# Turning a mixture layer's results with TensorE instead of with a transposing DMA

## The chip, the cores and the metric

The kernel runs on one core of a Trainium2 chip. The metric is the device time of one execution in microseconds (us); lower is better. Times "of a run" are medians of several executions of the same kernel; the profile is one further execution.

## The reference

Windowed attention with 4 batches, 8 heads, 576 positions and a head dimension of 64 gives 2304 rows of 512 values. Two mixture layers follow. In each a row picks one of 8 experts by the largest of its router logits, goes through that expert's two matrices, and is scaled by its gate:

```python
logits = x @ w_gate                      # layer 2: + modality_bias[modality_id]
e_idx = np.argmax(logits, axis=1)
...
h = np.maximum(x[mask] @ w1[e], 0.0)     # 512 -> 1024
ye = h @ w2[e]                           # 1024 -> 512
out[mask] = gate_w[mask, None] * eom[mask, e, None] * ye   # layer 2: without eom
```

The second layer's router needs the first layer's result of each row, so every result of layer 1 is also multiplied by the second `w_gate`. All products run on pairs of float16 values (a high and a low part), which keeps float32 accuracy.

## The kernel before

After attention the rows are sorted by expert into **slots** of 128 rows that share one expert. Each mixture layer is a loop over slots (`moe`, `slot(s)`); 18 slots are always there, up to 9 more run if the sort fills them. In the profiled execution slots 0 to 22 of layer 1 ran, and then the second layer's slots.

The order of all work is written out by hand: what the program says first on an engine runs first there, and each engine waits for its own next instruction. In a slot of layer 1 this order is:

- SyncE (SP) issues the loads of the next experts' weights into a float32 buffer `raw` (line 91) as soon as the splits of earlier pieces have read it. The loads are conditional: they move data only where the expert changes.
- ScalarE (ACT) splits the high part of the weights (line 99) and VectorE (DVE) the low part (line 104) into one of two buffers `wb`. A slot has four such places, `sp(0)` to `sp(3)`.
- `post.out(s - 1, py)` takes the previous slot's product out of PSUM: ACT scales it into `y` (line 996) and casts its high half into the tile `y16` (line 997), GpSimd (POOL) copies the row numbers (line 990) and subtracts for the low half (line 998). There is one `y16` for all slots but slot 1.
- TensorE (PE) makes the first product, `mm1` (line 797): twice 48 matmuls, each group into its own bank. After the first group SP gets `post.transposes(s - 1)`: a transposing DMA of `y16` into `yT` (line 1003) and a DMA of `y16` to the DRAM table `y_dram` (line 1004), out of which layer 2 gathers its rows. Behind them stands the transposing DMA of the next slots' inputs, `xT` (line 770).
- PE makes the second product, `mm2` (line 864), 12 float16 and 8 float32 matmuls, and then the router of an older result (`post.router`, line 1017, 12 small matmuls out of `yT`): in slots up to 16 that of two slots ago, from slot 17 on that of the slot before. DVE adds it to the logits (line 1025).

`post.transposes(None)` for the very last slot of layer 1 already turns with PE: eight transposes of 128x128 into the PSUM tile `pyt` (line 1008) and one DVE copy into `yT` (line 1009). The PSUM tag `pyt` has one buffer; the search for layer 2's first expert (`first_expert`, its `pfe2` tile, written at the end of slot 3 and read by DVE lines 169 and 170 in slot 4) uses it too.

`Fill` (lines 914 to 941) loads and splits, from slot 5 to 16, the first expert of layer 2 in the gaps. `hook(k)` are the places where such side work is hung in.

Of the kernel before, what the change touches and what calls it, by code (L numbers as in the profile page):

```python
# [20 lines left out]
N, DM, E, F = 2304, 512, 8, 1024  # L21
# [8 lines left out]
CA1, CA2, CF = 13, 13, 4  # L30
KA, KE = 2, 3
NMIN = 18
NB = 12
BIG = 8e12
SQK = 2.0 ** 5
# [13 lines left out]
def fused(ctx, tc, qk, vw, wr1, w1a, w2a, mid, wr2, mbias, w1b, w2b, cf, c16, cbs, cms, cib, out, dbg=None):  # L49
    nc = tc.nc  # L50
# [26 lines left out]
    def plain(wb):  # L77

        return [wb[:, i, UF * 512:].bitcast(F32) for i in range(2)]

    def load_raw(w1, w2, ev, cond=None, pieces=range(8), wb=None):

        kw = {} if cond is None else dict(cond=cond, cond_hint=False)
        for k in pieces:
            if k < 4:
                src = w1[bass.ds(ev, 1), k * P:(k + 1) * P, :].rearrange("e p f -> p (e f)")
                d = raw[:, k * 1024:(k + 1) * 1024]
            else:
                src = w2[bass.ds(ev, 1), 2 * (k - 4) * P:2 * (k - 3) * P, :].rearrange("e (c p) f -> p (e c) f", p=P)
                d = (raw[:, k * 1024:(k + 1) * 1024] if wb is None else plain(wb)[k - UF // 2]).rearrange("p (c f) -> p c f", c=2)  # L90
            nc.sync.dma_start(d, src, **kw)
# [484 lines left out]
    vt, gt = nc.vector, nc.gpsimd  # L576
# [173 lines left out]
    def moe(w1, w2, tab, src, parts, post, start, wfirst):  # L750


        xg, xs, regs, evr = {}, {i: xsA[i] for i in range(KA)}, [], {}
        one = post is post1
        npc = UF // 2 if one else 8
        py = pp.tile([P, DM], F32, name="py", tag="py")
        pys = [pp.tile([P, DM], F32, name=f"pya{i}", tag=f"pya{i}") for i in range(KA)]

        def gather(s):
            if s >= NSLOT:  # L760
                return
            t = xgb[s % 3][:, 0:src.shape[1]]
            nc.gpsimd.indirect_dma_start(t, None, src, bass.IndirectOffsetOnAxis(start.idx[:, s:s + 1], 0))  # L763
            xg[s] = t

        def x_transpose(s):
            if s >= NSLOT:
                return
            g = xg.pop(s)
            nc.sync.dma_start(xsb[s % 3], g[:, 0:8 * P], transpose=True)  # L770
            xs[s] = xsb[s % 3]
            post.gathered(s, g)

        def weights(s, pieces=range(8), always=False):
            if s >= NSLOT:
                return
            if not regs or regs[2] != s:
                regs[:] = (nc.sync.value_load(tab[0:1, 0, s:s + 1], min_val=0, max_val=E - 1),
                           None if always else nc.sync.value_load(tab[0:1, 1, s:s + 1], min_val=0, max_val=1), s)
                evr[s] = regs[0]  # L780
            load_raw(w1, w2, regs[0], cond=regs[1], pieces=[k for k in pieces if k < npc])

        def plains(s):

            if s < NSLOT and one:
                c = None if s < KE + 2 else nc.sync.value_load(tab[0:1, 2, s:s + 1], min_val=0, max_val=1)
                load_raw(w1, w2, evr.pop(s), cond=c, pieces=range(npc, 8), wb=wbuf[s % 2])

        def mm1(g, w1h, w1l, xT, mid):
            ph = pp.tile([P, 4, P], F32, name=f"ph{g}", tag=f"ph{g}")  # L790
            k = 0
            for w, b_ in ((w1h, (0, 4)), (w1l, (0,))):
                for j in range(4):
                    fs = slice((4 * g + j) * P, (4 * g + j + 1) * P)
                    for c in range(4):
                        for i in b_:
                            nc.tensor.matmul(ph[:, j, :], w[:, c, fs], xT[:, parts[c + i], :], start=k == 0, stop=k == 47, skip_group_check=True)  # L797
                            k += 1
                if k == 32:
                    mid()  # L800
            return ph

        def hsplit(g, ph, hh, hl):
            if one and g == 1:
                nc.scalar.activation(hh, ph, AF.Relu, scale=SW)  # L805
                return
            hs = hh[:, 4 * g:4 * g + 4, :]
            nc.scalar.activation(hs, ph, AF.Relu)  # L808
            nc.vector.scalar_tensor_tensor(out=hl[:, 4 * g:4 * g + 4, :], in0=ph, scalar=0.0, in1=hs, op0=ALU.max, op1=ALU.subtract)  # L809

        def slot(s):
            wb = wfirst if s < KE else wbuf[s % 2]
            w1h, w1l = (wb[:, i, 0:4096].rearrange("p (c f) -> p c f", c=4) for i in range(2))
            w2h, w2l = (wb[:, i, 4096:].rearrange("p (c f) -> p c f", c=8) for i in range(2))
            xT = xs.pop(s)

            def sp(i):
                if KE <= s < NSLOT - 1:
                    splits(wbuf[(s + 1) % 2], MO['ta1' if one else 'ta'][i], lambda k: weights(s + 2, k))

            def hook(k):
                start.hook(s, k)

            if s >= KE:
                gather(s + 2)
            hh = mp.tile([P, 8, P], F16, name="hh")
            hl = mp.tile([P, 8, P], F16, name="hl")
            if one:

                hf, hl = hl.rearrange("p f t -> p (f t)").bitcast(F32).rearrange("p (f t) -> p f t", f=4), hh[:, 4:8, :]  # L830
                if s >= KE - 1:
                    plains(s + 1)
            hook(0)
            sp(0)
            if s >= KE:
                post.out(s - 1, py)
            if s >= NMIN - 1 and post is not post1:
                post.now(s)
            sp(1)
            ph0 = mm1(0, w1h, w1l, xT, lambda: hook(1))  # L840
            hook(2)
            if s == NMIN - 1:
                post.router(s - 2)
            if s >= KE:
                post.transposes(s - 1)
            if s >= KA:
                x_transpose(s + 2)
            hsplit(0, ph0, hh, hl)
            sp(2)
            hook(3)  # L850
            ph1 = mm1(1, w1h, w1l, xT, lambda: hook(4))
            hsplit(1, ph1, hf if one else hh, hl)
            hook(5)
            sp(3)
            k = 0
            to = pys[s] if s < KA else py
            if one:
                wf = [t.rearrange("p (f d) -> p f d", d=DM) for t in plain(wb)]
                ops = [(hh[:, f, :], w[:, f, :]) for f in range(4) for w in (w2h, w2l)] + [(hl[:, f, :], w2h[:, f, :]) for f in range(4)]
                ops += [(hf[:, f, :], wf[f // 2][:, f % 2, :]) for f in range(4)]  # L860
            else:
                ops = [(a[:, f, :], w[:, f, :]) for a, b_ in ((hh, (w2h, w2l)), (hl, (w2h,))) for f in range(8) for w in b_]
            for a, w in ops:
                nc.tensor.matmul(to, a, w, start=k == 0, stop=k == len(ops) - 1)  # L864
                k += 1
                if k == 12:
                    hook(6)
            if s >= NMIN - 1:
                post.router(s - 1)
            elif s >= KE - 1:  # L870
                post.router(s - 2)
            hook(7)

        start.gather, start.transpose, start.weights, start.pys = gather, x_transpose, weights, pys
        start.first_splits = lambda o: splits(wbuf[KE % 2], o, lambda k: weights(KE + 1, k))
        for s in range(NMIN):
            slot(s)
            if s == KE - 1:
                nsl = nc.values_load(tab[0:1, 0, 31:32], min_val=1, max_val=NSLOT)
        with ExitStack() as ifs:  # L880
            for s in range(NMIN, NSLOT):
                ifs.enter_context(tc.If(nsl > s))
                slot(s)
        return py
# [60 lines left out]
    class Start1(Start):  # L945
# [16 lines left out]
        def zero(self, i):  # L962

            nc.sync.dma_start(y_dram[(NMIN + i) * P:(NMIN + i + 1) * P, :], zt)

# [12 lines left out]
    class Post1:  # L978
# [21 lines left out]
        def transposes(self, s):  # L1000
            y16 = self.row(s)
            if s is not None:
                nc.sync.dma_start(self.yT[s % 2], y16[:, 0:2 * DM], transpose=True)
                nc.sync.dma_start(y_dram[s * P:(s + 1) * P, :], y16)
                return
            pt = pp.tile([P, 8, P], F16, name="pyt", tag="pyt")
            for c in range(8):
                nc.tensor.transpose(pt[:, c, :], y16[:, c * P:(c + 1) * P], identh)
            vt.tensor_copy(self.yT[0], pt)

        def router(self, s):
            pl = pp.tile([P, E], F32, name="plg", tag="plg")
# [201 lines left out]
```

## Time and profile before

| | us |
|---|---|
| median of 3 runs | 700.32 |
| lowest and highest of them | 699.58, 705.36 |
| the profiled execution, its own time | 707.08 |
| its span, first to last instruction | 705.3 |
| slots 3 to 22 of layer 1 | from 207.59 to 467.75 in the span |

Over the span PE is busy 87%, DVE 74%, ACT 62%, POOL 56%; these are averages over stages (attention up to about 167 us, layer 1, and layer 2 from about 468 us). In the page's 40 slices of 17.6 us the DMA engines are busy nine tenths or more in most of the first half. In rows of instructions, "idle before" is what that engine waited for. A DMA's row on SP is the time SP's queue took to issue it, not its transfer.

### The profile page before, as it was taken

The numbers are of one execution on the slowest core, as the hardware profiler recorded it, in microseconds if no ns is written. First come the engines' busy times: TensorE is split into PE (matmuls) and PEld (weight loads), VectorE is DVE, ScalarE is ACT, GpSimd is POOL, SyncE is SP. The second block draws the span as 40 slices with busy tenths as digits, with TensorE's granted clock in tenths as the row PEclk, the third lists the DMA queues.
The fourth block names the chain that finished last, engine by engine and source line by source line (L and its number), as shares of the span: only waits on it lengthen the run. The fifth ranks groups of instructions, "written<-read, shape, count | busy, mean of one in ns | idle before, by whom it ended". The sixth has DMA issues, their size and how long they took to land. (4 is left out here: it accounts for less than half of the span.)

```text
span 705.3 us, 18714 instructions
## 1 busy us (share of the span) xinstructions
PE 611.9 (87%) x7180; PEld 460.6 (65%) x7180; DVE 524.5 (74%) x658; ACT 440.5 (62%) x529; POOL 394.1 (56%) x396
## 2 busy tenths in 40 slices
PE   3889888745999988999998979989799987999993
PEld 2788778745676755586755756766676764776771
DVE  4599797776449555686868845759399987999995
ACT  4588676551266556586867546631389866889883
POOL 2477676442462465666766822312679946666772
PEclk9999998956999998999999999999999998999997
DMA  9999999866867999999999599430953299233231
GB/s 204 222 214 226 231 247 244 252 211 185 238 175 172 298 259 316 298 224 307 233 273 236 121 227 230 100 65 20 290 82 105 77 307 290 47 79 92 62 76 47
DMA packets 134484, 133.72 MB, mean 190 GB/s; under 512 B 94447, under 2 KB 99311, under 8 KB 133360
## 3 DMA queue, kind: packets, MB, share of 16 engines
q1 hardware_dynamic: 128704, 114.56, 64.4%
q0 software_dynamic: 5280, 17.13, 8.4%
q8 instruction: 60, 0.98, 0.6%
q10 hardware_dynamic: 400, 0.72, 0.5%
q14 instruction: 40, 0.33, 0.2%
HBM read 209.91 MB, written 18.22 MB: 323 GB/s over the span
## 5 line engine op out<-in xcount | busy, mean ns | idle before, releaser
L104 DVE SCALAR_TENSOR_TENSOR wb<-raw,wb 128x1024 f16<-128x1024 f32 (+2 forms) x190 | 327.3, 1751 | 83.3 <-ACT wb L99 79.4
L99 ACT ACTIVATE wb<-raw 128x1024 f16<-128x1024 f32 (+1 forms) x190 | 256.9, 1399 | 65.2 <-DMA raw<-in_w1a 36.8
L797 PEld LDWEIGHTS <-wb 128*128 128x128 f16 x4032 | 231.4, 99 | 12.7 <-DMA xT<-xg 4.1
L797 PE MATMUL ph<-xT,wb 128*128 128x128 f16 x3648 | 213.0, 220 | 3.6 <-DMA xT<-xg 3.6
L864 PE MATMUL py<-wb,hh 128*128 128x512 f16 x524 | 122.1, 385 | 13.5 <-ACT hh L808 11.5
L864 PE MATMUL py<-wb,hl 128*128 128x512 f32 (+1 forms) x304 | 111.7, 508 | 7.3 <-ACT hl L805 6.5
L864 PEld LDWEIGHTS <-hh 128*128 128x128 f16 x580 | 55.0, 99 | 75.6 <-ACT hh L808 12.9
L808 ACT ACTIVATE hh<-ph 128x512 f16<-128x512 f32 x61 | 36.3, 595 | 47.1 <-PE ph L797 44.9
L864 PEld LDWEIGHTS py<-wb,hl 128*128 128x128 f32 x168 | 32.6, 196 | 42.8 <-issue 31.8
L990 POOL COPY y<-idxaa 128x1 int32<-128x1 int32 x21 | 16.9, 806 | 77.2 <-DMA y_dram<-y 77.0
L403 PE MATMUL po<-v,pT 128*96 128x65 f32 x384 | 42.6, 266 | 2.1 <-DMA v<-in_vw 2.1
L107 POOL TENSOR_SCALAR lotmp<-raw 128x512 f32<-128x512 f32 x17 | 30.8, 1810 | 19.8 <-DMA raw<-in_w1b 18.8
L763 POOL DMA_INDIRECT xg<-x_dram,idxaa x23 | 37.1, 1615 | 8.3 <-DVE e2a L677 4.2
L108 POOL TENSOR_TENSOR wb<-lotmp,wb 128x512 f16<-128x512 f32 x17 | 30.2, 1775 | 20.1 <-issue 17.9
L403 PEld LDWEIGHTS po<-v,pT 128*96 128x96 f32 x384 | 39.5, 182 | 2.4 <-DMA v<-in_vw 2.4
L998 POOL TENSOR_TENSOR y<-y,y 128x512 f16<-128x512 f32 x21 | 32.3, 1539 | 14.8 <-ACT y L997 13.3
L1106 POOL DMA_INDIRECT out<-y,idx x18 | 32.9, 1829 | 8.0 <-DMA raw<-in_w2b 5.2
L344 DVE TENSOR_REDUCE M<-ps 96x4 f32<-96x512 f32 x48 | 31.6, 679 | 5.0 <-PE ps L343 4.9
L301 DVE SCALAR_TENSOR_TENSOR kl<-qk,kh 128x608 f16<-128x608 f32 x32 | 29.9, 937 | 6.3 <-ACT kh L298 6.3
L342 PE MATMUL ps<-kh,qs 128*96 128x128 f16 x192 | 31.6, 240 | 3.0 <-ACT kh L298 2.9
L392 ACT ACTIVATE pT<-pst 128x384 f32<-128x384 f32 x48 | 23.5, 489 | 16.2 <-PE pst L391 15.6
L809 DVE SCALAR_TENSOR_TENSOR hl<-ph,hh 128x512 f16<-128x512 f32 x38 | 25.7, 678 | 10.3 <-ACT hh L808 10.3
(358 smaller groups left out, 896.3 us busy)
## 6 DMA issues: line engine op xcount, KB each, us to landing
raw<-in_w1a SPq DMA_DIRECT2D x92, 512.0 KB
raw<-in_w1b SPq DMA_DIRECT2D x72, 512.0 KB
raw<-in_w2b SPq DMA_DIRECT2D x72, 512.0 KB
raw<-in_w2a SPq DMA_DIRECT2D x46, 512.0 KB
wb<-in_w2a SPq DMA_DIRECT2D x44, 512.0 KB
qk<-in_qk SPq DMA_DIRECT2D x16, 608.0 KB
v<-in_vw SPq DMA_DIRECT2D x16, 390.0 KB
y_dram<-y SPq DMA_DIRECT2D x21, 260.0 KB
```

The lines of the kernel that those rows point to most:

```text
L99: nc.scalar.activation(wb[:, 0, s], raw[:, s], AF.Copy, scale=SW)
L104: nc.vector.scalar_tensor_tensor(out=wb[:, 1, s], in0=raw[:, s], scalar=SW, in1=wb[:, 0, s], op0=ALU.mult, op1=ALU.subtract)
L107: nc.gpsimd.tensor_scalar(pool[:, 0:n * 512], raw[:, s], SW, None, op0=ALU.mult)
L342: nc.tensor.matmul(ps[:, j, :], st, kh[:, h, QT * i:QT * i + 128], start=False, stop=False, skip_group_check=True)
L344: nc.vector.tensor_reduce(out=Ms[n][:, 4 * g:4 * g + 4], in_=ps, axis=AX.X, op=ALU.max)
L403: nc.tensor.matmul(po[:, i, :], pT[:, NQ * h + i, :], v[:, h, i, :], start=True, stop=True)
L763: nc.gpsimd.indirect_dma_start(t, None, src, bass.IndirectOffsetOnAxis(start.idx[:, s:s + 1], 0))
L797: nc.tensor.matmul(ph[:, j, :], w[:, c, fs], xT[:, parts[c + i], :], start=k == 0, stop=k == 47, skip_group_check=True)
L808: nc.scalar.activation(hs, ph, AF.Relu)
L864: nc.tensor.matmul(to, a, w, start=k == 0, stop=k == len(ops) - 1)
L998: gt.tensor_tensor(y16[:, DM:2 * DM], self.y, y16[:, 0:DM], op=ALU.subtract)
L1106: gt.indirect_dma_start(out, bass.IndirectOffsetOnAxis(idx2[:, s:s + 1] if s is not None else ilast, 0), y, None, bounds_check=N - 1, oob_ ...
```

## The change

Results 0 and 1 are still turned by DMA. Each result from number 2 on is turned by PE in the next slot, after that slot's `mm1` and before its `mm2`, into `pyt`, and copied into `yT` by DVE. The DMA to `y_dram` stays. The file has eleven lines more, so line numbers of the changed kernel are higher.

```diff
+TURN = KE - 1
...
             ph1 = mm1(1, w1h, w1l, xT, lambda: hook(4))
             hsplit(1, ph1, hf if one else hh, hl)
+            if one and s >= KE:
+                post.turn(s - 1)
             hook(5)
             sp(3)
...
         def transposes(self, s):
             y16 = self.row(s)
             if s is not None:
-                nc.sync.dma_start(self.yT[s % 2], y16[:, 0:2 * DM], transpose=True)
+                if s < TURN:
+                    nc.sync.dma_start(self.yT[s % 2], y16[:, 0:2 * DM], transpose=True)
                 nc.sync.dma_start(y_dram[s * P:(s + 1) * P, :], y16)
                 return
+            self.turn(s)
+
+        def turn(self, s):
+
+            if s is not None and s < TURN:
+                return
+            y16 = self.row(s)
             pt = pp.tile([P, 8, P], F16, name="pyt", tag="pyt")
             for c in range(8):
                 nc.tensor.transpose(pt[:, c, :], y16[:, c * P:(c + 1) * P], identh)
-            vt.tensor_copy(self.yT[0], pt)
+            vt.tensor_copy(self.yT[0 if s is None else s % 2], pt)
```

The program holds this for slots 3 to 26; of these, slots 3 to 22 ran in the profiled execution, so 20 transposing DMAs go and 20 turns come.

On SP, in slot 4, between the loads of `raw`, before:

```order
L91 DMA raw<-in_w1a 128x1024
L1003 DMA_TRANSPOSE yT_2803<-y_2797 128x8x128
L1004 DMA y_dram<-y_2797 128x1040
L770 DMA_TRANSPOSE xT_2784<-xg_2779 128x8x128
L91 ISA
L91 DMA raw<-in_w1a 128x1024
```

and of the change:

```order
L92 DMA raw<-in_w1a 128x1024
L1008 DMA y_dram<-y_2797 128x1040
L771 DMA_TRANSPOSE xT_2784<-xg_2779 128x8x128
L92 ISA
L92 DMA raw<-in_w1a 128x1024
```

One of the slot's two transposing DMAs is gone; the write of `y_dram` is issued in its place and everything behind it moves up.

On DVE, in slot 4, from the split of `mm1`'s first half to the router's sum, before:

```order
L809 SCALAR_TENSOR_TENSOR hh<-ph_3700,hh 128x512
L104 SCALAR_TENSOR_TENSOR wb_2766<-raw,wb_2766 128x1024
L169 TENSOR_REDUCE fe_m0b<-pfe_3658 128x1
L170 TENSOR_TENSOR fe_meb<-pfe_3658,fe_m0b 128x8
L171 TENSOR_TENSOR fe_meb<-fe_meb,cft 128x8
L172 TENSOR_REDUCE fe_mb<-fe_meb 128x1
L104 SCALAR_TENSOR_TENSOR wb_2766<-raw,wb_2766 128x1024
L104 SCALAR_TENSOR_TENSOR wb_2766<-raw,wb_2766 128x2048
L1025 SCALAR_TENSOR_TENSOR lg_77<-plg,lg_77 128x8
```

and of the change:

```order
L810 SCALAR_TENSOR_TENSOR hh<-ph_3709,hh 128x512
L105 SCALAR_TENSOR_TENSOR wb_2766<-raw,wb_2766 128x1024
L170 TENSOR_REDUCE fe_m0b<-pfe_3667 128x1
L171 TENSOR_TENSOR fe_meb<-pfe_3667,fe_m0b 128x8
L172 TENSOR_TENSOR fe_meb<-fe_meb,cft 128x8
L173 TENSOR_REDUCE fe_mb<-fe_meb 128x1
L1020 COPY yT_2803<-pyt 128x1024
L105 SCALAR_TENSOR_TENSOR wb_2766<-raw,wb_2766 128x1024
L105 SCALAR_TENSOR_TENSOR wb_2766<-raw,wb_2766 128x2048
L1036 SCALAR_TENSOR_TENSOR lg_77<-plg,lg_77 128x8
```

The copy out of `pyt` stands ahead of two weight splits; in this one slot it stands behind two readers of the tile `pfe`, which shares `pyt`'s PSUM buffer.

On PE, in slot 4 of the change, from the last matmul of `mm1` to the first of `mm2` (the pair of line 1019 stands eight times; before there was nothing between):

```order
L798 MATMUL ph_3771<-xT_2785,wb_69 128x128
L1019 LDWEIGHTS y_2797
L1019 MATMUL pyt<-identh,y_2797 128x128
...
L867 LDWEIGHTS hh
L867 MATMUL py<-wb_69,hh 128x512
```

PE now needs `y16` complete at this point of the slot.

## Rows read from the trace of the kernel before

**Rows 1.** The page: busy tenths of the DMA engines in 40 slices.
```profile
DMA  9999999866867999999999599430953299233231
```

**Rows 2.** Windows, core 0: slots 4, 5, 7, 16, 18, 19, 22, and sum of 20.
```profile
core 0: us, PE busy (x) PEld busy (x) DVE busy (x) ACT busy (x) POOL busy (x), PEclk, DMA share, GB/s
...
219.30:230.99 11.69, 11.69 (x135) 8.35 (x132) 10.21 (x17) 6.36 (x8) 5.53 (x7) 1.00 0.57 132
230.99:242.67 11.68, 11.68 (x134) 8.35 (x131) 5.92 (x8) 6.54 (x8) 5.50 (x5) 1.00 1.03 344
...
255.21:275.22 20.01, 14.85 (x134) 9.30 (x131) 9.68 (x8) 10.88 (x12) 9.35 (x7) 0.83 1.09 301
...
373.26:388.15 14.89, 12.51 (x160) 9.01 (x158) 12.47 (x15) 11.71 (x13) 8.91 (x8) 1.00 0.86 202
...
400.78:417.74 16.96, 11.87 (x134) 8.29 (x131) 7.90 (x6) 6.86 (x8) 3.98 (x3) 0.99 0.92 181
417.74:432.55 14.81, 13.38 (x135) 9.80 (x133) 7.31 (x6) 8.50 (x10) 4.44 (x3) 0.89 1.11 284
...
455.92:467.30 11.38, 11.38 (x123) 8.04 (x120) 7.89 (x6) 6.16 (x7) 2.36 (x2) 1.00 0.40 74
sum 259.71, PE 241.14 PEld 169.76 DVE 175.84 ACT 164.96 POOL 133.59; mean PE 12.06 PEld 8.49 DVE 8.79 ACT 8.25 POOL 6.68
```

**Rows 3.** Windows by stage: slots 6 to 16, and slots 17 to 22.
```profile
242.67:388.15 145.48, 133.90 (x1442) 93.26 (x1439) 100.47 (x87) 98.60 (x108) 90.69 (x58) 0.98 0.98 266
388.15:467.75 79.60, 72.60 (x786) 51.76 (x782) 49.98 (x39) 45.45 (x47) 29.73 (x22) 0.98 0.71 161
```

**Rows 4.** Waits from 207 to 470: us in total, times, longest.
```profile
POOL y L990 <- DMA y_dram<-y: 77.0, 15, 12.6
ACT wb L99 <- DMA raw<-in_w1a: 36.5, 11, 6.7
PE plg L1017 <- DMA yT<-y: 7.0, 3, 5.1
```

**Rows 5.** Tile yT and line 1008: duration ns min/median/max, first and last start.
```profile
L1003 SPq DMA_TRANSPOSE yT<-y x21: 1250/1261/3246, 200.2 to 459.6; - x21
L1008 PE MATMUL pyt<-identh,y x8: 217/219/219, 471.7 to 472.1; 128*128 128x128 f16 x8
L1009 DVE COPY yT<-pyt x1: 692/692/692, 472.4 to 472.4; 128x1024 f16<-128x1024 f16 x1
```

**Rows 6.** Timeline of PE: start, duration, what, idle before.
```profile
224.66 2.75 PE L864 MATMUL py<-wb,hh 128*128 128x512 f16 x12
...
248.87 2.76 PE L864 MATMUL py<-wb,hh 128*128 128x512 f16 x12 [0.68 <-ACT hh L808]
...
393.81 2.75 PE L864 MATMUL py<-wb,hh 128*128 128x512 f16 x12
...
406.14 2.75 PE L864 MATMUL py<-wb,hh 128*128 128x512 f16 x12
...
471.71 0.61 PE L1008 MATMUL pyt<-identh,y 128*128 128x128 f16 x8
472.16 1.06 PE L797 MATMUL ph<-xsA,wb 128*128 128x128 f16 x16
```

**Rows 7.** Timeline of POOL, line 998: when `y16` was complete in slots 6, 17, 18.
```profile
248.69 1.15 POOL L998 TENSOR_TENSOR y<-y,y 128x512 f16<-128x512 f32 x1
...
396.11 1.15 POOL L998 TENSOR_TENSOR y<-y,y 128x512 f16<-128x512 f32 x1
...
403.48 1.15 POOL L998 TENSOR_TENSOR y<-y,y 128x512 f16<-128x512 f32 x1
```

**Rows 8.** Timeline of DVE (slots 4 and 22) and ACT (slot 19).
```profile
225.86 0.17 DVE L170 TENSOR_TENSOR fe_meb<-pfe,fe_m0b 128x8 f32<-128x8 f32 x1
...
463.05 1.22 DVE L104 SCALAR_TENSOR_TENSOR wb<-raw,wb 128x1024 f16<-128x1024 f32 x1 [1.45 <-ACT wb L99]
...
418.92 0.62 ACT L997 CAST y<-y 128x512 f16<-128x512 f32 x1
```

## The prediction, made before the change was run

> **What bounds the kernel now.** The chain of waits says nothing here (it reaches back only over the last few instructions), so I read layer 1 slot by slot. The page's DMA line [rows 1] is the first hint: nine tenths and more in most of layer 1. Next, the windows cut at the start of each slot's first product [rows 2]. A slot in which PE never stops takes 11.69 us, and PE is busy in all of it (slots 4 and 5): that is the floor, and PE sets it. Twenty slots, 3 to 22, took 259.71 us; 20 x 11.69 = 233.8, so **25.9 us are stalls**. Where they lie: slots 6 to 16 took 145.48 us against 11 x 11.69 = 128.6, 16.9 too many, with the DMA engines 0.98 busy; slots 17 to 22 took 79.60 against 70.1, 9.5 too many [rows 3]. The largest are slot 7 (8.3 over the floor, granted clock 0.83, so part of it ran at 1.2 GHz), slot 16 (3.2), slot 18 (5.3) and slot 19 (3.1, clock 0.89) [rows 2].
>
> Then the waits of that stretch [rows 4]: ACT waited 36.5 us for weights from DMA, POOL 77.0 us for the write of y_dram to land before it could write y16 again, and PE itself 7.0 us in three places for yT from the transposing DMA, once 5.1 us. So in slots 6 to 16 PE waits for ACT, ACT for DMA queues that are full; in 17 to 19 PE waits for the very transfer that the change removes.
>
> **The change part by part.**
>
> *Eight transposes on PE per slot.* In the last slot, where PE already turns, the eight begin at 471.71 and the next matmul at 472.16 [rows 6]: 0.45 us of PE, though each lasts 219 ns by itself [rows 5], since they overlap. 20 x 0.45 = **+9.0 us** on the engine that sets the floor; the new floor of a slot is 12.14. The Trainium skill ("TensorE: Matmul & The Clock Gate", Part 4) says that a PE transpose of 128x128 took 390 ns alone and about 275 ns within a kernel; read as a cost per transpose that would be 8 x 0.275 = 2.2 us a slot. The trace has less.
>
> *The DVE copy*, 0.69 us [rows 5], 20 of them. In an undisturbed slot DVE idles 1.45 us before the next split because ACT has not made the high part yet [rows 8], and the copy fits in it: nothing. DVE is busy 175.84 of 259.71 us [rows 2], so 13.8 us more is no bound. If the cover goes (ACT early), a split is up to 0.69 late, which delays a load, not PE.
>
> *The shared PSUM buffer, slot 4.* The turn cannot write pyt before DVE's line 170 has read pfe, which ended at 225.86 + 0.17 = 226.03; PE got there at 224.66 [rows 6, 8]. **+1.4 us**, once. Behind it PE holds mm2 only.
>
> *The new wait for y16.* PE now needs y16 at the end of mm1, and mm2 is queued behind it. Before, y16 was complete later than PE could have used it, and not hidden by another wait of the same slot, in six of the slots 6 to 17, by 8.5 us in all, from slot 6 (248.69 + 1.15 = 249.84 against 248.87) to slot 17 (397.26 against 393.81) [rows 6, 7]. In slots 6 to 16 the reason is mostly POOL's wait for the y_dram write [rows 4], and this write now leaves one transposing DMA earlier: at least the 1.25 us that SP's queue takes to issue one [rows 5], plus its transfer. That covers most of these 5.0 us; I leave 1.0. In slot 17 POOL is late because of its own list (gathers and the index sums of layer 2's first slots), so there I take 2.0 out of 0 to 3.5. **+3.0 us.**
>
> *One DMA less per slot.* What a transposing DMA costs the 16 engines has no row of its own. From below: 1.25 us, the time to issue it. From above: slot 22 loads nearly no weights and holds two of them, one y_dram write and a gather in 0.40 x 11.38 = 4.6 us [rows 2], so less than 2.3. I take 1.5, near the lower end, because the y_dram write and the gather must have their share of the 4.6. Over 11 slots that frees 16.5 us of the full queues, about the 16.9 us of stalls. It cannot remove all: transposes in stretches where the queue ran empty buy nothing, and slot 7 stalled 8.3 us, of which two slots' transposes are 3.0 and the lost clock (0.17 x 20.01 = 3.4) comes back only if the wait becomes short. I leave 2.0 in slot 7 and 1.5 in slot 16, where index work of layer 2 is part of it. **-13.4 us**; bounds 0 and -16.9. The Trainium skill ("Advanced Engine Details and Errata", X-Bar Transpose) says that transposing DMAs on this chip are as fast as ordinary ones. In slot 22 the engines moved 74 / 0.40 = 185 GB/s while busy, in slot 5, full of weights, 344 / 1.03 = 334: the trace disagrees. By that rule 256 KB would take 0.8 us, and 11 slots would free 8.6 us instead of 16.5.
>
> *Slots 17 to 19.* PE's waits for yT go: 7.0 [rows 4]. y16 of slot 18 was ready at 404.63, before mm1's end at 406.14 [rows 6, 7], so there the turn is free of waiting. The low clock of slot 19 followed the 5.1 us wait; without it 0.11 x 14.81 = 1.6 come back. Late next is y16 in slot 19: ACT, behind a weight load, finished its half at 419.54 [rows 8], POOL needs 1.15 more, and PE, starting slot 19 5.1 earlier than 417.74 and with 5.4 of mm1 (219.30 to 224.66 in slot 4), would be there at about 418.0: some 2.6. **-8.6 + 2.6 us.**
>
> Sum: 9.0 + 1.4 + 3.0 - 13.4 - 8.6 + 2.6 = **-6.0 us**. Against the profiled execution's own 707.08 that is 701.1. That execution lies 6.8 us above the median of 700.32 (one of the three runs, 705.36, lay near it). No trace shows where the faster ones saved it; if part was in these stalls, there is less to win. I therefore take 5.3 off the median: **695.0 us**. One per cent, 7 us, is about what tells a change from none here: below 693.3 is faster, above 707.3 slower.
>
> **The rivals.**
>
> *The forecast (0.45):* stalls shrink by more than the turns add, 691 to 697.
>
> *The queues run free (0.22).* If all stalls of slots 6 to 19 go but the fixed side work, the gain is 25.9 - 9.0 - 1.4 = 15.5 less about 1: 684 to 690. For it: freed 16.5 against stalled 16.9. Against it: loads come in bursts.
>
> *Hidden anyway (0.20).* If the weight loads themselves set the stalls (an expert change moves 4 MB, and the transposes only fill holes), slots 6 to 16 keep theirs. The turns are then free in the slots that stall, six of these eleven, and cost 14 x 0.45 = 6.3; 6.3 + 1.4 + 2.0 - 8.6 + 2.6 = +3.7: 700 to 706, middle 704. For it: slot 5 moved 344 GB/s, so weights alone can fill the queues.
>
> *PE waits for POOL (0.11), the slower side.* The turn puts ACT, POOL and a DMA write onto PE's path in the middle of each slot. If the y_dram write lands no earlier, all 8.5 us of late y16 fall on PE: 9.0 + 1.4 + 8.5 - 8.6 + 2.6 = +12.9, 713. It decides where y16 is complete later than 5.4 us after a slot's start in more than a few slots. Against it: SP issues the write at least 1.25 us sooner.
>
> *The transposes do not overlap (0.02).* Eight at 219 ns would be 1.75 us a slot, 35.0 instead of 9.0: 721. The last slot's rows speak against it. The reading of the skill's Part 4 above would be this case with 44 us.
>
> That the transfers do not leave the program is excluded by the order on SP.
>
> From these: faster 0.22 and about a third of the forecast's own range, 0.38; slower 0.13; the rest 0.49. The range leaves out the slower side and the lowest part of the free-queue case: 686 to 706; the forecast's own is 691 to 697.
>
> **What would show it.** Right: slots without a stall take about 12.1 us; PE's wait for yT is gone; POOL's wait for y_dram falls well below 77 us; ACT's for w1a well below 36.5; the transposes idle less than 5 us in all on y16, most of it in slot 17. Wrong: slots 6 to 16 still take about 145 us with the DMA share near 1 (hidden anyway), or PE rows at the turn with idle time released by POOL line 998 in many slots, and a granted clock below 1 after them (POOL), or slots of 13.4 us with no wait (no overlap).

## The result and the profile after

The change took **691.46 us** (median of 4 executions, 689.63 to 692.47) against 702.84 of the kernel before (699.58 to 705.7): ratio **0.984**, 95% interval 0.980 to 0.988, so it is faster by over 1%. The prediction was 695.0 in a range of 686 to 706, with 0.49 on "within 1%" and 0.38 on "faster", which is what came. A second comparison of the same two kernels (e8) gave 0.984 [0.981, 0.987]. The ratios here and below leave out an execution over 1.5% above the fastest of its kernel (one each of e2, e6, e10 and e12, that of e6 at 1371.63 us, and three of before), the medians include it.

The profiled execution of the change has an own time of 689.63, the lowest of its four, and a span of 687.9, 17.4 below the span of before, whose 707.08 lies above all four of its runs. Not all of the 17.4 is the change's: slot 3, ahead of which both programs are the same, began at 203.31 instead of 207.59 (4.28). In the fourteen profiles of this study it began anywhere between 202.16 and 207.59. So I compare stretches. Slots 3 to 22, up to the end of the last router, took 248.10 instead of 260.16 us, **12.06 less**; the rest after them 1.1 less.

Windows of the change, columns as in [rows 2]: slots 4, 7, 9, 16 and 19, then the two stages of [rows 3]:

```profile
215.47:229.01 13.54, 12.29 (x142) 8.84 (x139) 10.71 (x18) 8.08 (x9) 6.48 (x8) 1.00 0.59 173
...
253.27:265.41 12.14, 12.14 (x143) 8.80 (x140) 9.63 (x8) 10.22 (x12) 7.21 (x5) 1.00 1.13 344
...
277.54:290.52 12.98, 12.30 (x142) 8.80 (x139) 7.96 (x7) 8.47 (x10) 7.02 (x5) 1.00 1.07 327
...
364.14:378.02 13.88, 12.96 (x168) 9.46 (x166) 12.36 (x16) 10.99 (x12) 9.85 (x8) 1.00 0.57 143
...
402.73:414.87 12.14, 12.14 (x143) 8.81 (x140) 7.24 (x7) 8.97 (x9) 3.15 (x3) 1.00 1.13 327
...
241.14:378.02 136.88, 134.67 (x1530) 97.51 (x1527) 111.90 (x97) 97.02 (x106) 88.68 (x58) 1.00 0.88 254
378.02:451.41 73.39, 73.38 (x834) 53.16 (x830) 52.65 (x45) 45.56 (x46) 25.11 (x21) 1.00 0.58 153
```

A slot without a stall takes 12.14 now, the 11.69 of before and 0.45. Slot 7 is such a slot (20.01 before), slot 19 too (14.81). The granted clock is 1.00, the level of 2.4 GHz, in every slot. By stage:

| slots | before | change | difference | predicted difference |
|---|---|---|---|---|
| 3 to 5 | 35.08 | 37.83 | +2.75 | +2.75 (3 x 0.45 + 1.4) |
| 6 to 16 | 145.48 | 136.88 | -8.60 | -7.45 (11 x 0.45 + 1.0 - 13.4) |
| 17 to 22 | 79.60 | 73.39 | -6.21 | -1.3 (6 x 0.45 + 2.0 - 8.6 + 2.6) |
| all | 260.16 | 248.10 | -12.06 | -6.0 |

The waits of the change from 207 to 455, columns as in [rows 4]:

```profile
POOL y L993 <- DMA y_dram<-y: 42.2, 13, 7.7
...
ACT wb L100 <- DMA raw<-in_w1a: 16.5, 10, 4.4
```

Both are about half of [rows 4], and PE's wait for yT is not among the waits of this kernel. What came in its place is in PE's timeline (the turns of slots 4, 9, 10, 12 and 16; of slot 12 also the matmul behind):

```profile
222.24 0.61 PE L1019 MATMUL pyt<-identh,y 128*128 128x128 f16 x8 [1.25 <-DVE fe_meb L171]
...
283.96 0.40 PE L1019 MATMUL pyt<-identh,y 128*128 128x128 f16 x4 [0.68 <-POOL y L1001]
...
296.88 0.40 PE L1019 MATMUL pyt<-identh,y 128*128 128x128 f16 x4 [0.61 <-POOL y L1001]
...
320.93 0.61 PE L1019 MATMUL pyt<-identh,y 128*128 128x128 f16 x8
321.37 2.75 PE L867 MATMUL py<-wb,hh 128*128 128x512 f16 x12
...
370.81 0.40 PE L1019 MATMUL pyt<-identh,y 128*128 128x128 f16 x4 [0.92 <-POOL y L1001]
```

From 320.93 to 321.37 eight transposes hold PE for 0.44 us. Slot 4 waits for the shared PSUM buffer, and three slots wait for the low half of `y16`, 2.21 us in all. (The first four transposes of such a slot need only the high half, which ACT writes, and go ahead.)

### The profile page after: what moved, and what is told of

Its sections match the earlier page's. It is cut to its first block, busy times and chain, and to the rows that moved or that the text cites. A ratio compares the mean times of both kernels' runs of the same rounds, so it can differ in the third digit from the quotient of the medians.

```text
span 687.9 us, 19033 instructions
## 1 busy us (share of the span) xinstructions
PE 607.9 (88%) x7340; PEld 459.8 (67%) x7340; DVE 541.0 (79%) x678; ACT 441.8 (64%) x529; POOL 397.9 (58%) x396
## 5 line engine op out<-in xcount | busy, mean ns | idle before, releaser
L100 ACT ACTIVATE wb<-raw 128x1024 f16<-128x1024 f32 (+1 forms) x190 | 257.1, 1400 | 38.1 <-DMA raw<-in_w1a 16.9
L867 PE MATMUL py<-wb,hl 128*128 128x512 f32 (+1 forms) x304 | 109.2, 497 | 2.1 <-DVE hl L810 2.1
L1001 POOL TENSOR_TENSOR y<-y,y 128x512 f16<-128x512 f32 x21 | 39.2, 1867 | 42.8 <-ACT y L1000 39.0
L404 PE MATMUL po<-v,pT 128*96 128x65 f32 x384 | 38.9, 252 | 0.7 <-DMA v<-in_vw 0.6
L764 POOL DMA_INDIRECT xg<-y_dram,idxbb x19 | 35.1, 1845 | 7.1 <-DVE e2b L678 4.0
L993 POOL COPY y<-idxaa 128x1 int32<-128x1 int32 x21 | 14.1, 672 | 42.3 <-DMA y_dram<-y 42.2
L404 PEld LDWEIGHTS po<-v,pT 128*96 128x96 f32 x384 | 35.8, 168 | 1.1 <-DMA v<-in_vw 1.0
L312 ACT ACTIVATE qs<-qk 64x576 f16<-64x576 f32 x32 | 21.6, 681 | 18.8 <-DMA qk<-in_qk 14.5
```

The costliest lines, as they stand in the source:

```text
L100: nc.scalar.activation(wb[:, 0, s], raw[:, s], AF.Copy, scale=SW)
L404: nc.tensor.matmul(po[:, i, :], pT[:, NQ * h + i, :], v[:, h, i, :], start=True, stop=True)
L1001: gt.tensor_tensor(y16[:, DM:2 * DM], self.y, y16[:, 0:DM], op=ALU.subtract)
```

## The experiments

**Theory:** the gain comes from the time that the transposing DMAs took of the 16 engines, which delayed the weights. **Rivals:** the place in SP's queue or the cost of issuing them; the single `y16` that stays busy until they have read it; PE's own waits for yT in slots 17 to 19. Ratios are against the kernel before, run beside each. The stages are those of one profile each, in us, and vary from one profile to the next: the change itself took 136.88 and, in e8, 138.86 in slots 6 to 16.

| run | 6 to 16 | 17 to 22 | median | ratio [95%] |
|---|---|---|---|---|
| e1 unread transposing DMA added | 146.61 | 73.39 | 701.25 | 1.000 [0.997, 1.004] |
| e2 ordinary copy of the same size | 137.67 | 73.39 | 695.2 | 0.987 [0.978, 0.995] |
| e3 ordinary copy of 16 B a partition | 137.73 | 73.64 | 693.22 | 0.987 [0.981, 0.993] |
| e4 turns from result 16 on only | 144.46 | 78.22 | 702.05 | 0.999 [0.995, 1.002] |
| e5 turns up to result 15 only | 136.67 | 76.00 | 693.77 | 0.986 [0.982, 0.991] |
| e6 every turn twice | 140.10 | 76.87 | 701.29 | 0.996 [0.993, 0.999] |
| e7 turn within mm2 in slots 3 to 16 | 136.88 | 74.63 | 692.39 | 0.984 [0.981, 0.987] |
| e8 the change again | 138.86 | 73.38 | 691.8 | 0.984 [0.981, 0.987] |
| e9 before, with two `y16` | 141.81 | 78.22 | 701.6 | 0.999 [0.995, 1.002] |
| e10 e1 with two `y16` | 148.84 | 73.40 | 699.2 | 0.993 [0.989, 0.998] |
| e11 change with two `y16` | 138.33 | 73.76 | 694.6 | 0.985 [0.980, 0.991] |
| e12 e11, result taken out earlier | 138.69 | 74.33 | 693.76 | 0.982 [0.977, 0.987] |

### Three transfers put back, e1 to e3

Each adds a DMA that nobody reads, on SP, where the transposing DMA stood. Into a scratch tile it reads `y16` in full with the transposition (e1), in full without (e2), or its first 8 values a partition (e3).

```diff
+                else:
+                    nc.sync.dma_start(self.spare, y16[:, 0:2 * DM], transpose=True)          # e1
+                    nc.sync.dma_start(self.spare.rearrange("p c t -> p (c t)"), y16[:, 0:2 * DM])   # e2
+                    nc.sync.dma_start(self.spare.rearrange("p c t -> p (c t)")[:, 0:8], y16[:, 0:8])  # e3
```

> The changed kernel plus a transposing DMA of each result 2 to 21 into a tile that nobody reads, at the place where the old one stood. PE turns as in the change. Theory (the gain in slots 6 to 16 is the transfer that is gone, with what it held up): slots 6 to 16 take 142 us or more instead of 136.9, the kernel is 6 to 14 us slower than the changed one, while slots 17 to 22 stay within 2 us of 73.3. Rival (the gain is only that PE no longer waits for yT): within 2 us of the changed kernel.

> As the first, but the unread transfer is an ordinary copy of the same 256 KB. If the transposing is what is dear (half the rate of ordinary loads), about half of what the transposing one gives back, 3 to 7 us slower than the changed kernel. If it is one more transfer in the queue whatever its kind, as much as that one.

> As the first, but the unread transfer is 16 bytes per partition: it takes SP's issue and a place in the queue and moves nothing to speak of. If bytes and packets count: within 2 us of the changed kernel. If SP's issue or the number of transfers in flight counts: 3 us or more slower, close to the ordinary copy.

e1 gives the whole gain back, though nobody reads what it moves. Its waits in slots 6 to 16, then those of the change in the same slots:

```profile
POOL y L994 <- DMA y_dram<-y: 42.9, 11, 8.9
ACT wb L100 <- DMA raw<-in_w1a: 25.4, 9, 5.3
...
POOL y L993 <- DMA y_dram<-y: 11.8, 6, 3.7
ACT wb L100 <- DMA raw<-in_w1a: 11.3, 7, 4.4
```

Share times length is the time that the packets took, as time of all 16 engines. (A share above 1, such as the 1.13 of slot 7, says that packets overlap in it.) Over slots 3 to 22, in which the programs differ by twenty transposing DMAs, it is in before, the change, e1 and e2:

```profile
207.59:467.75 260.16, 241.58 (x2607) 170.11 (x2603) 175.84 (x163) 164.96 (x176) 133.59 (x93) 0.98 0.88 230
...
203.31:451.41 248.10, 244.63 (x2767) 177.15 (x2763) 194.03 (x183) 166.66 (x176) 128.56 (x93) 1.00 0.79 220
...
205.59:463.42 257.83, 247.68 (x2767) 177.71 (x2764) 191.19 (x183) 165.73 (x176) 125.98 (x93) 0.99 0.89 232
...
205.27:454.16 248.89, 244.66 (x2767) 177.09 (x2764) 192.73 (x183) 166.46 (x176) 126.72 (x93) 1.00 0.83 240
```

That is 0.88 x 260.16 = 228.9 us before, 196.0 in the change, 229.5 in e1. Worked out in the same way, the profiles with all twenty (before, e1, e9, e10) have 221.9 to 231.4, mean 227.9; those with none of them (the change, e6, e7, e8, e11, e12) 193.8 to 198.5, mean 196.3. So (227.9 - 196.3) / 20 = **1.6 us per transposing DMA**; the extreme profiles would give 1.2 and 1.9. For e2 it is 206.6, so (206.6 - 196.3) / 20 = **0.5 us for the same 256 KB copied straight**, in this one profile. The pages' packet counts show how the two transfers differ (the change, e1, e2):

```profile
DMA packets 113366, 128.50 MB, mean 187 GB/s; under 512 B 73327, under 2 KB 78191, under 8 KB 112240
...
DMA packets 134485, 133.74 MB, mean 191 GB/s; under 512 B 94447, under 2 KB 99311, under 8 KB 133360
...
DMA packets 116245, 133.74 MB, mean 193 GB/s; under 512 B 73647, under 2 KB 78511, under 8 KB 115120
```

Each transposing DMA moves its 256 KB in 1,056 packets under 512 B, each of e2's copies in 16 such and 128 of 2 KB or more.

e2 and e3 cannot be told apart, and their slots 6 to 16 are as in the change. (The median of e2 is 3.7 us above that of the change, which would be the 3 to 7 that I expected, but the interval of its ratio, 0.978 to 0.995, leaves open whether that is real.) So neither one more transfer in the queue nor its bytes takes the gain back; what the transposing adds does. It adds two things, and these runs do not separate them:

- Time of the engines, 1.6 against 0.5 us, in many small packets. An ordinary copy in packets as small was not tested.
- Time of SP's queue, in which the loads of `raw` stand behind it. Its own issue takes 1.26 us against 0.50 for e2's copy, and that of the next transposing DMA, `xT`, grows too. Its durations in slots 6 to 16 (ns: lowest, median, highest) of before, e1, e2 and the change:

```profile
L770 SPq DMA_TRANSPOSE xT<-xg x12: 1290/2826/3564, 243.1 to 384.7; - x12
...
L771 SPq DMA_TRANSPOSE xT<-xg x12: 1290/2336/3223, 242.1 to 385.7; - x12
...
L771 SPq DMA_TRANSPOSE xT<-xg x11: 1270/1853/2822, 250.3 to 374.8; - x11
...
L771 SPq DMA_TRANSPOSE xT<-xg x11: 1256/1538/2172, 248.1 to 371.2; - x11
```

That SP came late to the loads shows in what it waited for in these slots. In the change it stood 16.0 us until DVE had freed a piece of `raw`, so those loads left as soon as they could; before it hardly ever had to (e1 0.3, e2 4.6, e3 10.7 us). Before, then the change:

```profile
SPq L91 <- DVE wb L104: 1.9, 3, 0.8
...
SPq L92 <- DVE wb L105: 16.0, 12, 2.0
```

### One part of the change alone, e4 and e5

```diff
-TURN = KE - 1
+TURN = 16                                    # e4: results 2 to 15 stay with the DMA
+TEND = 16                                    # e5: only results 2 to 15 are turned by PE
-                if s < TURN:
+                if not TURN <= s < TEND:     # e5, and the same in turn()
```

> Only results 16 and later are turned by PE (slots 17 to 22), the others by DMA as before. Theory: slots 6 to 16 stall as before (about 145 us), slots 17 to 22 take about 73 to 75 instead of 79.6; 695 to 698 against 702.8 before. Rival (the late waits would come back as other waits): no faster than 701.

> Results 2 to 15 are turned by PE (slots 3 to 16), results 16 and later by DMA as before. If the transposing DMAs of slots 6 to 16 are what stalls there: slots 6 to 16 take 136 to 139 us as in the change, and the waits for yT at the end of slots 17 to 19 come back (5 to 7 us, less 6 x 0.45 of turns saved): 694 to 697. Rival (the late waits went because everything before ran on time): slots 17 to 22 within 1 us of the changed kernel's 73.3, and 690 or less.

e4 is no faster than before, as the rival had it. PE waits no more for yT, but in slot 17 it waits for POOL. PE there, then POOL's list:

```profile
390.81 0.39 PE L1019 MATMUL pyt<-identh,y 128*128 128x128 f16 x4
394.32 0.40 PE L1019 MATMUL pyt<-identh,y 128*128 128x128 f16 x4 [3.12 <-POOL y L1001]
394.56 4.44 PE L867 MATMUL py<-wb,hh 128*128 128x512 f16 x12
```

```profile
377.69 2.04 POOL L1001 TENSOR_TENSOR y<-y,y 128x512 f16<-128x512 f32 x1 [2.50 <-ACT y L1000]
...
383.42 1.24 POOL L241 TENSOR_SCALAR ea_cons<-rc 128x13 f32<-128x13 f32 x1
384.75 2.06 POOL L242 TENSOR_TENSOR ea_consr<-ea_cons,rc 128x13 f32<-128x13 f32 x1
...
393.12 1.15 POOL L1001 TENSOR_TENSOR y<-y,y 128x512 f16<-128x512 f32 x1
```

The row of mm2 behind the wait, 4.44 us instead of 2.75, is at the lower clock; the slot's window says what that cost:

```profile
385.16:402.57 17.41, 14.29 (x154) 9.54 (x151) 9.74 (x10) 7.34 (x9) 11.54 (x8) 0.90 0.46 115
```

In e5 slots 6 to 16 are as in the change, and PE waits for yT again in slots 18 and 19 (the router's rows):

```profile
404.85 0.46 PE L1029 MATMUL plg<-wr2h,yT 128*128 128x8 f16 x12 [1.61 <-DMA yT<-y]
...
418.57 0.46 PE L1029 MATMUL plg<-wr2h,yT 128*128 128x8 f16 x12 [1.86 <-DMA yT<-y]
```

So the early part alone already brings these waits down from 7.0 [rows 4] to 3.5. Against before, e5 gains 8.8 us in slots 6 to 16 and 3.6 in 17 to 22; with the late part as well it is 2.6 more there, while the late part alone gains 1.4. By medians e5 cannot be told from the change.

### The price of the turn, e6

```diff
-            for c in range(8):
+            for c in list(range(8)) * (1 if s is None else 2):
```

The second eight write the same values again.

> The changed kernel with each of the 20 turns done twice on PE (16 transposes into the same tile). If a turn costs 0.45 us of PE on the path in every slot: slots without a stall take 12.57 instead of 12.13 and slots 3 to 22 are 8 to 9 us longer, about 700. Rival (transposes do not overlap, or run at the lower clock): 13 us or more per slot.

A turn and the first matmul behind it:

```profile
327.11 1.06 PE L1019 MATMUL pyt<-identh,y 128*128 128x128 f16 x16
328.00 2.75 PE L867 MATMUL py<-wb,hh 128*128 128x512 f16 x12
```

Sixteen hold PE for 0.89 us, twice 0.45: the price grows in step, with no fixed part to speak of. Slots 6 to 16 became 3.2 us longer than in the change, rather than 11 x 0.45 = 5.0: PE gets to the turn later in each slot, and the waits for `y16` of slots 9 and 10 are gone. The ratios agree with the price: 0.996 against the 0.984 of e8 beside it is 1.2%, some 8 us, against 20 x 0.45 = 9.0.

### The turn elsewhere, e7; the change again, e8

e7 does the turn of slots 3 to 16 after the twelve float16 matmuls of mm2, and gives `pfe2` another PSUM tag.

```diff
+                    if one and KE <= s < NMIN - 1:
+                        post.turn(s - 1)
-... name="pfe2", tag="pyt"), fe2)
+... name="pfe2", tag="pw"), fe2)
```

> The changed kernel with the turn of slots 3 to 16 moved into mm2, after its 12 float16 matmuls, and layer 2's pfe2 tile in another PSUM buffer. The four waits at the turn (1.25 in slot 4, 0.68, 0.61 and 0.92 in slots 9, 10 and 16) go: 3 to 3.5 us faster than the changed kernel, 687 to 689. Rival (something else is late in the same slots: the weights' halves or hh): under 1.5 us faster, other waits in those slots.

> The changed kernel again, beside the others, to compare with: 690 to 692.5.

The waits of slots 4 and 16 are gone in e7, and yet it is no faster than the change. Two places of slot 9, and slot 11:

```profile
284.27 2.76 PE L867 MATMUL py<-wb,hh 128*128 128x512 f16 x12 [1.25 <-ACT hh L809]
...
287.97 3.70 PE L867 MATMUL py<-wb,hl 128*128 128x512 f32 x8 [0.49 <-ACT hl L806]
```

```profile
304.00:316.19 12.19, 12.19 (x143) 8.77 (x139) 11.16 (x10) 8.73 (x10) 11.75 (x6) 1.00 0.77 206
```

An undisturbed slot costs 0.05 more (12.19 in slot 11), slot 9 stalls on ACT instead, and slot 17 waits 1.11 for POOL. A wait taken away at one point of PE was replaced by the next late operand.

### A second `y16`, e9 to e12

Odd results after the first go through a second tile, so that POOL need not wait for the write of y_dram: in before (e9), in e1 (e10), in the change (e11, there with `pfe2` moved as in e7). e12 is e11 with `post.out` put ahead of the slot's first weight split.

```diff
-            return xg2[0] if s == 1 else y16s
+            return xg2[0] if s == 1 else zt if s is not None and s % 2 else y16s
...
+            if one and s >= KE:              # e12, ahead of sp(0)
+                post.out(s - 1, py)
```

> The kernel before with two tiles for y16, used in turn, so that a result no longer waits for the last one's write to y_dram. If the transposing DMA harms by keeping the one y16 busy: 5 us or more faster than before, and slots 6 to 16 at 139 us or less. If it harms by the time that it takes from the weight loads: within 3 us of before, slots 6 to 16 above 141, ACT still waiting over 20 us for w1a there.

> The first experiment (PE turns, an unread transposing DMA stays) with two tiles for y16. If the harm is the busy y16: its 9.7 us in slots 6 to 16 fall below 3. If it is the time taken from the weight loads: 6 us or more of them stay, now as waits for ACT (hh, hl) in place of waits for POOL at the turn.

> The changed kernel with two tiles for y16 and pfe2 in another PSUM buffer. The waits at the turn for POOL go where POOL waited for y_dram (slots 9 and 10, 0.6 to 1.7 us), that of slot 4 (1.25) goes, that of slot 16 (0.92) may stay: 2 to 4 us faster than the changed kernel, 687.5 to 689.5. Rival (weights late in slot 9 anyway, as in the seventh run): about 1.3 us.

> The kernel of the run before (two tiles for y16, pfe2 elsewhere), and in each slot of layer 1 ACT takes the last result out of PSUM before the first weight split of the slot, not after it. If the waits at the turn in slots 9 and 10 come from ACT standing behind a weight load, they go (1.3 to 2.5 us) and slots 6 to 16 take 135.5 to 137; slot 16's, behind layer 2's index work, goes or shrinks too. Rival (the splits, now later, stall mm2's float32 half in the same slots): slots 6 to 16 at 138 or more, as in the run before.

In e9 the medians show no gain, though this profile's slots 6 to 16 are 3.7 us shorter. ACT's wait for weights in its slots 6 to 16 stays (e9, then before):

```profile
ACT wb L99 <- DMA raw<-in_w1a: 28.0, 9, 6.8
...
ACT wb L99 <- DMA raw<-in_w1a: 26.6, 8, 5.2
```

In e10 less than half of the change's gain came back, 0.7% against 1.6%. Against e11, which lacks the unread DMA, e10 is 0.8% slower by these ratios and 10.5 us longer in slots 6 to 16. So the busy `y16` is not the whole harm. By the ratios it can be about half of what e1 lost; in the kernel before, by e9, freeing it is worth 0.1%, and at most 0.5% by the interval. In e11 PE still waits at the turn (slot 9 1.65, slot 10 0.88, slot 16 1.06), though POOL waits for no write of y_dram there. ACT and then POOL in its slot 9:

```profile
282.48 1.91 ACT L100 ACTIVATE wb<-raw 128x2048 f16<-128x2048 f32 x1 [5.32 <-DMA raw<-in_w1a]
```

```profile
285.70 2.03 POOL L1001 TENSOR_TENSOR y<-y,y 128x512 f16<-128x512 f32 x1 [5.84 <-ACT y L1000]
```

In slot 9 `y16` is late because ACT takes the result out only behind a split whose weights are late. e12 turns that order round; PE and ACT in slot 9:

```profile
284.94 0.61 PE L1021 MATMUL pyt<-identh,y 128*128 128x128 f16 x8
...
290.51 5.40 PE L869 MATMUL py<-wb,hl 128*128 128x512 f32 x8 [2.37 <-ACT hl L806]
```

```profile
287.88 1.06 ACT L100 ACTIVATE wb<-raw 128x1024 f16<-128x1024 f32 x1 [3.57 <-DMA raw<-in_w1a]
```

The turn of slot 9 waits no longer, and the same late weights now hold `hl`, another operand out of ACT; the clock granted over these eight matmuls was 0.68. What is left of slot 9 is the load of that expert. No version here can be told from the change as faster.

## Why the prediction was right, point by point

Direction and range were right; the gain is twice what I forecast, 11.4 us in medians instead of 5.3. That the time still fell into the forecast's own 691 to 697 is partly luck: I took the 5.3 off a median of 700.32, which one more execution moved to 702.84, and from there the same sum gives 697.5.

- **The turn, +9.0:** right. 0.44 us a turn in the change, 0.89 for a double one in e6, and undisturbed slots of 12.14. The reading of "TensorE: Matmul & The Clock Gate", Part 4 of the Trainium skill, as a cost per transpose (2.2 us a slot) does not agree: a single one lasts 219 ns here too [rows 5], but eight in a row overlap.
- **The DVE copy, 0, and slot 4, +1.4:** right; undisturbed slots hold nothing of the copy, slot 4 waits 1.25.
- **One DMA less, -13.4:** right in its cause, the transposing DMA, shown by e1 to e3, and a little small. In slots 6 to 16 the change stands at 136.88 against 11 x 12.13 = 133.4; 2.2 of these 3.5 are waits at the turn, so of the old 16.9 us 1.2 are left, most of it further matmuls of slot 16 (PE is busy for 12.96 of its 13.88 us), and 15.7 are gone. In e8, the same kernel, 2.4 are left and 14.5 gone. A transposing DMA takes 1.6 us of the engines, near my 1.5, though the time to issue it, from which I took the lower bound, is SP's time and not theirs. I left too much in slot 7, which has no stall now, and I put the time that SP's queue loses at nothing, where the issue of `xT` alone went from a median of 2.83 us to 1.54. The rule of "Advanced Engine Details and Errata", X-Bar Transpose, in the Trainium skill (as fast as ordinary DMAs) is not borne out here: 1.6 against 0.5 us of the engines for the same bytes.
- **The wait for y16, 1.0 in slots 6 to 16:** 2.2 (3.1 in e8), and for another reason than I gave. I had named the write of y_dram; e11 has no wait for it and the turns still wait. In slot 9 ACT's output stands behind late weights, in slot 16 ACT had stood 4.13 us for DVE's index work of layer 2. And in each of the three slots POOL's subtraction of the low half was long. DVE and POOL in slot 9 of the change:

```profile
280.60 2.29 DVE L105 SCALAR_TENSOR_TENSOR wb<-raw,wb 128x2048 f16<-128x2048 f32 x1 [2.72 <-ACT wb L100]
```

```profile
281.88 2.03 POOL L1001 TENSOR_TENSOR y<-y,y 128x512 f16<-128x512 f32 x1 [2.30 <-ACT y L1000]
```

  The subtraction ended at 283.91, 1.02 after the weight split of DVE that was running when it began, and so it did in slots 10 (2.51 us long) and 16 (2.03). In all fourteen profiles, from 195 to 470 us, the 112 subtractions that began while no split ran took 1.14 to 1.17 us, and 166 of the 179 that began during one took 1.9 to 3.1. With 1.15 each, at most 0.04 of the 2.21 us of waits would be left; no run here changes that alone.
- **The two waits in slots 17 and 19, +2.0 and +2.6:** this is the step that failed, 4.6 of the 4.9 us by which slots 17 to 22 beat the forecast. In slot 17 I kept POOL's lateness of before, as if slot 16 did not change. From one `y16` to the next POOL needed 14.54 in e4 (379.73 to 394.27) and PE 12.64 from the start of mm2 to the end of mm1, so POOL falls back by 1.9. It also began 1.56 behind, since mm2 of slot 16 started at 378.17 without waiting for `y16`. In the change the turn of slot 16 makes PE wait (0.92), mm2 starts at 371.04, after `y16` (370.75), and POOL's list is shorter:

```profile
374.40 0.57 POOL L241 TENSOR_SCALAR ea_cons<-rc 128x13 f32<-128x13 f32 x1
375.06 1.00 POOL L242 TENSOR_TENSOR ea_consr<-ea_cons,rc 128x13 f32<-128x13 f32 x1
...
382.83 1.16 POOL L1001 TENSOR_TENSOR y<-y,y 128x512 f16<-128x512 f32 x1
```

  370.75 to 383.99 are 13.24 us, and PE is at the turn at 383.68: nearly no wait. So one short wait in slot 16 and a list 1.3 us shorter stand for the long wait in slot 17. The two index sums (lines 241 and 242) take 1.57 here and 3.30 in before, e4, e7 and e9, the four profiles without a turn between mm1 and mm2 of slot 16. In those four a weight split of DVE was already running when the first sum began (in e4 from 382.36, the sum from 383.42); here the turn's copy delays DVE, and the split began after it (374.77 against 374.40). It looks like the same hold-up as with the subtraction, but no run tests it.
- In slot 19 ACT waited 6.72 us for w1a before; in the change it waits 2.83 and `y16` is ready at 407.58, ahead of the turn at 408.09. My +2.6 moved PE forward by 5.1 us and left the load where it was.
- **Slots 17 to 19, -8.6:** the stalls there went, all of them (73.39 against 6 x 12.13 = 72.8), but they are not separate from slots 6 to 16: e5 halves PE's waits for yT without touching these transfers, and e4, which removes them, turns them into a wait for POOL.
- **The discount from -6.0 to -5.3** went the wrong way. The medians show 11.4 of the profiles' 12.06.

Of the rivals, "the queues run free" (0.22) came nearest to the profiles; its price of 14.5 was too large by 2.4, about the turn waits of 2.2. "PE waits for POOL" is what e4 shows, in one slot only.

## What to carry to other kernels

Where the DMA queues are full, price a transfer by the time it takes of the engines (share of a stretch times its length, with it and without it) and by how long it holds the queue that issues it, not by its bytes. A term that keeps a wait from the old trace has to say what that wait is measured from: when the stage ahead moves, the lateness of the next operand moves too. Compare stretches between fixed points of the program, because here the part ahead varied by up to 5 us between executions of the same code.

## What the runs showed of the hardware that was not expected

- A transposing DMA of 256 KB took about 1.6 us of all 16 engines, in 1,056 packets under 512 B; an ordinary copy of the same bytes took about 0.5.
- Where a transposing DMA stood close ahead of it in SP's queue, the issue of the next one took a median of 2.34 to 2.87 us in slots 6 to 16 (before, e1, e9, e10), otherwise 1.34 to 1.85 (the change, e2, e3, e8).
- POOL's subtraction of 128x512 took 1.14 to 1.17 us when no weight split ran on DVE as it began, and 1.9 to 3.1 in 166 of the 179 cases in which one did.
- Added transposing DMAs that nobody reads cost 7.8 to 9.7 us in eleven slots with full queues (e1 with 146.61, the change with 136.88 and 138.86) and nothing in six slots with room (73.39 in both).
- Slot 3 began between 202.16 and 207.59 us in the profiles although the same program ran ahead of it; the cause stays open.
